# A first stage in plain fp32, a third part out of the table, a threshold on ScalarE and a split of weights at the hand-over

## The chip, the cores and the metric

The kernel runs on one core of a Trainium2 chip. The metric is the device time of a whole execution in microseconds (us), lower is better; the change is judged by medians of several runs. The engines are named as in the profile: PE is TensorE (PEld its weight loads), ACT is ScalarE, DVE is VectorE, POOL is GpSimd, SP is SyncE, which only issues DMAs.

## The reference

Three layers in a row, cut to what matters. Eight batches of 3072 tokens of width 256 run through all of them.

```
X = rfft(x, axis=1)                              # 8 x 3072 x 256
Yr = Xr @ w_r - Xi @ w_i + b_r ;  Yi = Xr @ w_i + Xi @ w_r + b_i
Yr, Yi = soft threshold by 0.01: sign(Y) * max(|Y| - 0.01, 0)
x = irfft(Yr + i Yi).reshape(24576, 256)
logits = x @ phi                                 # 32 slots
d = softmax over the tokens ; slot_input = d.T @ x
slot_out = relu(slot_input @ w1[e]) @ w2[e]      # 8 experts, 4 slots each
y = softmax over the slots(logits) @ slot_out
h = y @ w_in ; g = h * tanh(log1p(exp(h)))
out = g @ w_out                                  # 2048 hidden columns
```

## The kernel before, in words

**The trunk** computes the transforms batch by batch. A batch has four groups, so there are 32 groups `k`. `stage1` multiplies twelve chunks of 512 columns of a batch by the 128 x 128 matrix `f1`; the result goes to DRAM (`sdr`) and comes back as `bt`, regrouped. In `stage1` both factors are split into a high and a low fp32r part (`xsplit`, lines 174 to 182), and three fp32r matmuls (high x high, low x high, high x low) make one product. `stage2` multiplies `bt` by a table `tall` of 96 columns per pair of frequencies, in plain fp32: 32 matmuls a group, four to a PSUM bank. Its 96 columns are a real and an imaginary part of 48 each. ScalarE writes the high part `xh`, VectorE the low part `xl`; both also add the two parts into `xsum` and split that as a third part (lines 228 to 236). `linear` makes the complex product with three real ones of six fp32r matmuls each, from those three parts, two output halves a group. The first of the three is copied by ScalarE (`k1`), the other two are added to it by VectorE (line 257), clamped by VectorE (259) and subtracted by POOL (260): the soft threshold. `special` repeats the first product for two columns of the first group of a batch, with eight plain fp32 matmuls.

`project` multiplies by `phi` for the logits, `ptrans` turns that with TensorE transposes, `inv1` transforms back, `uturn` turns again and stores to `udr`. Once a batch the softmaxes follow (`inv2`, `smax1` to `smax3`, `csoft1`, `csoft2`) and the sums over tokens (`fwd1`, `fwd2`, `dturn`, `slots`); `ytrans` makes the transposes of the thresholded columns that `slots` needs.

**Beside the trunk** `conv` turns the 64-bit weights `w_in` and `w_out` into fp32, in 32 pieces; the 16 of `w_out` are also split into high and low and stored to `whl_d` in DRAM.

**The tail**: the experts (`Experts.run`), then `ffn`. Here 384 blocks run a pipeline: `hidden` (line 774), `gate` (Mish on ScalarE, 780), `high` and `low` (785, 789: the split of the gate's output on VectorE), and `omm` (804), which multiplies by `whl`, the split of `w_out`; `omm` follows `hidden` by `LAG` = 3 blocks.

**What sets the order**: no scheduler. Each step is put on a list with a position by `at(pos, ...)`, in units of a group; the list is sorted and the instructions issued in that order, so every engine and SP's queue work strictly in it. A position is a place in the order, not a time. `PA` and `TAIL` hold the positions; `TAIL["loads"]` those of the experts' weights. The trunk's PSUM pool has 8 banks in rotation.

Of the kernel before, what the change touches and what calls it, by code (L numbers as in the profile page):

```python
# [8 lines left out]
F32 = mybir.dt.float32  # L9
# [19 lines left out]
def constants():  # L29
# [32 lines left out]
    both = np.concatenate([t.reshape(96, -1), tt.reshape(96, -1)], axis=1)  # L62
# [4 lines left out]
def body(ctx, tc, x, w_r, w_i, b_r, b_i, phi, w1, w2, w_in, w_out, cbig, ct, out, dbg=None, stop=False):  # L67
# [16 lines left out]
    whl_d = dram.tile([2, FF, D], F32, name="whl_d")  # L84
# [28 lines left out]
    f1s = [wp.tile([128, 128], F32R, name=f"f1s{i}") for i in range(2)]  # L113
# [11 lines left out]
    def setup():  # L125
# [19 lines left out]
    def weights():
# [14 lines left out]
        nc.vector.tensor_scalar(thi, bias, -1.0, LAM, op0=ALU.mult, op1=ALU.add)  # L160

    def load_t(i, g):
        w = 8 * 96
        o = (4 * i + g) * w
        nc.sync.dma_start(out=tall[:, o:o + w], in_=ct[:, o:o + w])

    def load_x(b, j):
# [696 lines left out]
```

## Time and profile before

| | us |
|---|---|
| median of 3 runs (2008.23 to 2022.46) | 2022.21 |
| profiled execution: its own time | 2017.93 |
| its span | 2016.0 |
| PE busy in the span | 1938.5 |
| PEld busy | 1643.8 |
| DVE busy | 1310.3 |
| ACT busy | 870.0 |
| POOL busy | 271.4 |

The profiled execution is 4 us under the median and inside the spread of the runs. Matmuls overlap, so a busy PE is not PE at its peak: what a matmul takes of PE is read from the distance between starts in the timeline. A plain fp32 matmul shows as two passes there (32 for the 16 that a call of `stage2` halves issues), an fp32r matmul or a transpose as one. PEclk is the share of full clock that PE was granted.

### The profile page before, as it was taken

What the parts mean: (1) busy time and instruction counts of PE and PEld (TensorE: products, weight loads), DVE (VectorE), ACT (ScalarE), POOL (GpSimd) and SP (SyncE); (2) the same over time, 40 slices, a digit from 0 to 9 for tenths busy, and PEclk for the clock granted to TensorE, in tenths of its full rate; (3) what the DMA queues carried; (4) which work ended last, traced back from release to release, by engine and by line L of the source; (5) the groups of instructions that cost most, each with busy time, mean ns of one, the idle gap of its engine ahead of it and who ended that gap; (6) DMA issues with size and microseconds to landing.
All of it is one profiled execution on the core that took longest, in us unless ns stands there. A gap on an engine that the chain in (4) does not pass through costs nothing.

```text
span 2016.0 us, 31876 instructions
## 1 busy us (share of the span) xinstructions
PE 1938.5 (96%) x12670; PEld 1643.8 (82%) x12670; DVE 1310.3 (65%) x2026; ACT 870.0 (43%) x1563; POOL 271.4 (13%) x289
## 2 busy tenths in 40 slices
PE   5999999999999779999999999999999999999999
PEld 3887787888888638888888888888888888888887
DVE  4777777787777535666666666666666666666665
ACT  4556565566655422333333333333333333333332
POOL 1443443444534100000000000000000000000000
PEclk7989999999999989999999999999999999999999
DMA  8655565666664691001002002002002002000000
GB/s 265 175 163 148 161 170 162 177 178 175 194 175 116 204 329 27 22 22 53 22 22 53 22 21 53 11 22 53 21 22 53 22 22 53 22 22 22 22 22 21
DMA packets 148388, 177.16 MB, mean 88 GB/s; under 512 B 57600, under 2 KB 102784, under 8 KB 147984
## 3 DMA queue, kind: packets, MB, share of 16 engines
q1 hardware_dynamic: 146448, 170.38, 28.7%
q0 software_dynamic: 1792, 4.76, 0.7%
q8 instruction: 100, 1.64, 0.3%
q14 instruction: 48, 0.39, 0.1%
HBM read 103.79 MB, written 71.30 MB: 87 GB/s over the span
## 4 chain that ended last, share of the span: by engine, by line
PE 65%; DMA 3%; DVE 2%; issue 1%; ACT 1%; POOL 1%; SPq 0%; POOLq 0%; DVEq 0%; ACTq 0%
PE o L804 53%; PE h L774 9%; DMA whl<-whl_d 1%; PE l L249 1%; DMA c_d<-chl 0%; PE s L221 0%; DMA raw<-in_moe_w_dram 0%; POOL yt L260 0%; DVE xl L229 0%; PE dt L446 0%; DVE xsum L230 0%; DVE rm L343 0%; ACT xh L235 0%; DVE p L257 0%; DVE cl L259 0%
## 5 line engine op out<-in xcount | busy, mean ns | idle before, releaser
L804 PE MATMUL o<-whl,gh 128*128 128x512 f32 x3072 | 1084.8, 396 | 7.3 <-DMA whl<-whl_d 7.3
L804 PE MATMUL o<-whl,gl 128*128 128x256 f32 x3072 | 828.7, 280 | 0.0
L780 ACT ACTIVATE g<-h 128x1024 f32<-128x1024 f32 x384 | 394.3, 1027 | 759.4 <-PE h L774 753.7
L804 PEld LDWEIGHTS o<-whl,gh 128*128 128x128 f32 x3072 | 567.5, 188 | 129.7 <-issue 8.0
L804 PEld LDWEIGHTS o<-whl,gl 128*128 128x128 f32 x3072 | 579.5, 189 | 31.5
L785 DVE CAST gh<-g 128x1024 fp32r<-128x1024 f32 x384 | 265.6, 692 | 366.7 <-ACT g L780 366.7
L789 DVE TENSOR_TENSOR gl<-g,gh 128x1024 fp32r<-128x1024 f32 x384 | 469.9, 1224 | 28.9 <-DVE gh L785 0.9
L774 PE MATMUL h<-ctt,mst 128*128 128x512 f32 x768 | 241.7, 396 | 1.8 <-DVE mst L766 0.9
L260 POOL TENSOR_TENSOR yt<-p,cl 128x384 f32<-128x384 f32 x126 | 134.6, 1068 | 219.0 <-DVE cl L259 113.1
L774 PEld LDWEIGHTS h<-ctt,mst 128*128 128x128 f32 x768 | 121.4, 189 | 20.4 <-DVE mst L766 1.9
L194 PE MATMUL s<-xsp,f1s 128*128 128x512 f32 x288 | 101.9, 455 | 29.7 <-ACT xsp L177 14.7
L221 PEld LDWEIGHTS s<-tall,bt 96*128 96x128 f32 x1024 | 127.1, 203 | 3.0 <-DMA bt<-sdr 2.3
L221 PE MATMUL s<-tall,bt 96*128 96x96 f32 x1024 | 126.5, 285 | 1.8 <-DMA bt<-sdr 1.8
L812 DVE TENSOR_TENSOR os<-o,os 128x256 f32<-128x256 f32 x192 | 76.3, 418 | 76.8 <-ACT os L811 76.8
L194 PEld LDWEIGHTS s<-xsp,f1s 128*128 128x128 f32 x288 | 53.5, 203 | 53.9 <-ACT xsp L177 19.7
L259 DVE TENSOR_SCALAR cl<-p,tlo,thi 128x384 f32<-128x384 f32 x128 | 76.9, 601 | 26.0 <-POOL yt L260 15.2
L811 ACT ACTIVATE os<-o 128x256 f32<-128x256 f32 x192 | 73.7, 384 | 41.0 <-PE o L804 38.0
L257 DVE TENSOR_TENSOR p<-l,k 128x384 f32<-128x384 f32 x128 | 70.3, 549 | 24.4 <-PE l L249 23.2
L229 DVE TENSOR_TENSOR xl<-s,xh 128x384 fp32r<-128x384 f32 x128 | 70.4, 550 | 17.6 <-ACT xsum L228 16.0
L235 ACT ACTIVATE xh<-xsum 128x384 fp32r<-128x384 f32 x64 | 33.5, 524 | 100.9 <-DVE xsum L230 100.9
L224 ACT ACTIVATE xh<-s 128x384 fp32r<-128x384 f32 x128 | 62.4, 487 | 33.6 <-PE s L221 33.6
L322 ACT ACTIVATE y<-tr 96x512 f32<-96x512 f32 x128 | 66.7, 598 | 17.2 <-PE tr L320 17.2
(190 smaller groups left out, 1914.8 us busy)
## 6 DMA issues: line engine op xcount, KB each, us to landing
xc<-in_x_dram SPq DMA_DIRECT2D x96, 256.0 KB, 3.1
sdr<-a SPq DMA_DIRECT2D x96, 256.0 KB, 3.4
bt<-sdr SPq DMA_DIRECT2D x32, 768.0 KB, 7.3
out_dram<-os SPq DMA_DIRECT2D x48, 512.0 KB, 2.6
ctt<-c_d SPq DMA_DIRECT2D x32, 384.0 KB, 7.9
c_d<-chl SPq DMA_DIRECT2D x16, 384.0 KB, 3.3
w1t<-in_moe_w_dram SPq DMA_DIRECT2D x6, 1024.0 KB, 7.6
w2t<-in_moe_w_dram SPq DMA_DIRECT2D x5, 1024.0 KB, 11.0
```

Of the source, the lines that this page charges most:

```text
L194: nc.tensor.matmul(ps, lhsT=f1s[w], rhs=xs[:, v], start=n == 0, stop=n == 2)
L221: nc.tensor.matmul(ps[:, i], lhsT=b_t[k][:, p0 + i, h * 128:(h + 1) * 128], rhs=t_m[:, 8 * g + p0 + i, :], start=True, stop=True)
L229: nc.vector.tensor_sub(xl_t[k][:, h, p0:p0 + 4, 0:2], ps, xh.bitcast(F32))
L259: nc.vector.tensor_scalar(cl, p, tlo[:, ri, eh:eh + 1], thi[:, ri, eh:eh + 1], op0=ALU.max, op1=ALU.min)
L260: (nc.vector if k == NK - 1 and m == 2 else nc.gpsimd).tensor_sub(yt[:, eh, :, ri, :], p, cl)
L774: nc.tensor.matmul(ps[:, i], lhsT=mst[:, f * 128:f * 128 + 128], rhs=ct_t[b][:, 4 * m:4 * m + 4].rearrange("p n t -> p (n t)"), start=True ...
L780: nc.scalar.activation(out=g, in_=h_t.pop(p), func=AF.Mish)
L785: nc.vector.tensor_copy(gh, g)
L789: nc.vector.tensor_sub(gl, g, gh.bitcast(F32))
L804: nc.tensor.matmul(o, lhsT=a[:, i, ts], rhs=w, start=f == 0 and n == 0, stop=f == 15 and n == 1)
L811: nc.scalar.activation(out=os[:, t], in_=ps[:, 1], func=AF.Copy)
L812: nc.vector.tensor_add(os[:, t], ps[:, 0], os[:, t])
```

## The change

- The table `t_m` gets 48 more columns for each pair of frequencies, the sum of the two parts. `stage2` writes 144 columns a matmul, three to a bank (banks of 3, 3 and 2 pairs, six a group for four before), and ScalarE and VectorE split all three parts at once. `xsum` and its four instructions go.
- `stage1` is one plain fp32 matmul of `x` and `f1`; `xsplit` goes. From the second batch on `x` is loaded and the result stored in pieces of 1024 columns, at positions of their own.
- The threshold is `relu(p + b - 0.01) - relu(-p - b - 0.01)`: two ScalarE activations with a bias for each clamp of VectorE; POOL subtracts as before.
- `special` has no matmuls: its two columns ride on the first product as columns 385 and 386.
- `project` writes frequencies onto partitions in three groups of 32, and VectorE transposes 32 x 32 blocks out of PSUM, in `project` and in `inv1`; `ptrans` and `uturn` with their TensorE transposes go. `udr` is stored by four DMAs of 32 partitions for two of 96.
- `conv` loads its piece earlier, into two buffers, and no longer splits `w_out`. `w_out` is fetched as fp32 into `wof` and split into `whl` by `split`, a quarter at each of the first four even blocks of `ffn`.
- The loads of the second expert's output weights come earlier, those of the fourth and fifth behind the last store of `c_d`. The first fetch of `ctt` is cut in two around `wof`.

```diff
-    both = np.concatenate([t.reshape(96, -1), tt.reshape(96, -1)], axis=1)
+    t3 = np.concatenate([t, t[:, :, 0:48] + t[:, :, 48:96]], axis=2)
+    both = np.concatenate([t3.reshape(96, -1), tt.reshape(96, -1)], axis=1)
...
-    tall = const.tile([96, NP * 192], F32, name="tall")
-    t_m = tall[:, 0:NP * 96].rearrange("p (n f) -> p n f", f=96)
-    t_t = tall[:, NP * 96:].rearrange("p (n f) -> p n f", f=96)
+    tall = const.tile([96, NP * 240], F32, name="tall")
+    t_m = tall[:, 0:NP * 144].rearrange("p (n f) -> p n f", f=144)
+    t_t = tall[:, NP * 144:].rearrange("p (n f) -> p n f", f=96)
...
+        nc.vector.tensor_scalar(tup, bias, -LAM, None, op0=ALU.add)
...
+        w = 8 * (96 if i else 144)
+        o = NP * 144 * i + g * w
...
+        w = XC if b == 0 else 2 * XC
...
+            c = slice(j % 2 * XC, j % 2 * XC + XC)
+            xs = x_t[b, j // 2][:, c]
+            if j % 2 == 0:
+                a_t[b, j // 2] = xp.tile([128, 2 * XC], F32, tag="a", name="a")
+            a = a_t[b, j // 2][:, c]
...
-        for n, (w, v) in enumerate(((0, 0), (1, 0), (0, 1))):
-            nc.tensor.matmul(ps, lhsT=f1s[w], rhs=xs[:, v], start=n == 0, stop=n == 2)
-        if j + 1 < na:
-            xsplit(b, j + 1)
-        elif b + 1 < NB:
-            xsplit(b + 1, 0)
+        nc.tensor.matmul(ps, lhsT=f1, rhs=xs, start=True, stop=True)
...
+    def store_a(b, i):
         dst = sdr[b].rearrange("q (r n) d -> (q r) (n d)", r=4)
-        nc.sync.dma_start(out=dst[:, j * XC:(j + 1) * XC], in_=a)
+        nc.sync.dma_start(out=dst[:, 2 * i * XC:2 * (i + 1) * XC], in_=a_t.pop((b, i)))
+        x_t.pop((b, i))
...
+        n = min(3, 8 - p0)
...
-        ps = psum([128, 4, 2, 48], "s2")
-        for i in range(4):
+            xh_t[k] = bp.tile([128, 2, 3 * NC + 2], F32R, tag="xh", name="xh")
+            xl_t[k] = bp.tile([128, 2, 3 * NC + 2], F32R, tag="xl", name="xl")
+        full = psum([128, 3, 3, 48], "s2")
+        ps = full[:, 0:n]
+        for i in range(n):
...
-        xh = xh_t[k][:, h, p0:p0 + 4, 0:2]
+
+        def part(t):
+            v = t[:, h, 0:3 * NC].rearrange("p (r q f) -> p q r f", r=3, f=48)
+            return v[:, p0:p0 + n]
+
+        xh = part(xh_t[k])
         nc.scalar.activation(out=xh, in_=ps, func=AF.Copy)
-        if p0 == 0:
-            k1_t["s", h] = lp.tile([128, 8, 48], F32, tag="xsum", name="xsum")
-        xs = k1_t["s", h]
-        nc.scalar.activation(out=xs[:, p0:p0 + 4], in_=ps[:, :, 0], func=AF.Copy)
-        nc.vector.tensor_sub(xl_t[k][:, h, p0:p0 + 4, 0:2], ps, xh.bitcast(F32))
-        nc.vector.tensor_add(xs[:, p0:p0 + 4], ps[:, :, 1], xs[:, p0:p0 + 4])
+        nc.vector.tensor_sub(part(xl_t[k]), ps, xh.bitcast(F32))
         if g == 0 and p0 == 0:
-            nc.vector.tensor_copy(xs_t[k][:, h, :], ps[:, 0, 0:2, 47])
...
+            for t in (xh_t[k], xl_t[k]):
+                nc.vector.tensor_copy(t[:, h, 3 * NC:3 * NC + 2], t[:, h, 47:48 + NC:NC].bitcast(F32))
...
-        ps = psum([128, 8, 48], "l")
+        w = NC + 2 if m == 0 and k % 4 == 0 else NC
+        full = psum([128, NC + 2], "l")
+        ps = full[:, 0:w]
+        cs = slice(src * NC, src * NC + w)
...
-        nc.vector.tensor_scalar(cl, p, tlo[:, ri, eh:eh + 1], thi[:, ri, eh:eh + 1], op0=ALU.max, op1=ALU.min)
-        (nc.vector if k == NK - 1 and m == 2 else nc.gpsimd).tensor_sub(yt[:, eh, :, ri, :], p, cl)
+        nc.scalar.activation(out=cl, in_=p, func=AF.Relu, bias=tup[:, ri, eh:eh + 1])
+        nc.scalar.activation(out=p, in_=p, func=AF.Relu, scale=-1.0, bias=tlo[:, ri, eh:eh + 1])
+        (nc.vector if k == NK - 1 and m == 2 else nc.gpsimd).tensor_sub(yt[:, eh, :, ri, :], cl, p)
...
-        ps = psum([128, 2], "sp")
...
+        v = k1_t[eh][:, NC:NC + 2]
...
-        ps = psum([128, 2, 96], "pp")
+        ps = psum([96, 8, NS], "pp")
         for eh in range(2):
...
-        pt_t[k] = turn(pt_t[k], "phat")
+            v = yt[:, eh].rearrange("p q r f -> p q (r f)")
+            for a in range(3):
+                nc.tensor.matmul(ps[32 * a:32 * a + 32], lhsT=ph[:, eh, :], rhs=v[:, :, 32 * a:32 * a + 32],
+                                 start=eh == 0, stop=eh == 1, tile_position=(0, 32 * a))
+        pt_t[k] = cp.tile([96, 8, NS], F32, tag="phat", name="phat")
+        nc.vector.transpose(out=pt_t[k].rearrange("p q s -> p (q s)"), in_=ps.rearrange("p q s -> p (q s)"))
...
+        u = cp.tile([128, 2, 3, NS], F32, tag="u", bufs=2, name="u")
+        nc.vector.transpose(out=u.rearrange("p i a s -> p (i a s)"), in_=ps.rearrange("p i f -> p (i f)"))
...
+        for j in range(4):
+            q = 8 * g + 2 * j
+            nc.sync.dma_start(out=udr[b][q:q + 2].rearrange("i (a n) s -> n i a s", n=32), in_=u[32 * j:32 * j + 32])
...
+            cv["n"] = cvp.tile([128, n, 2], I32, tag="cs", bufs=2, name="cvs")
+            nc.sync.dma_start(out=cv["n"], in_=srcd[i])
...
-            nc.sync.dma_start(out=whl_d[:, 128 * i:128 * i + 128].rearrange("r p d -> p r d"), in_=cv["hl"].bitcast(F32))
...
+        for i in range(na // 2 if b else 0):
+            at(4 * b + PA["s1"] + PA["s1d"] * (2 * i + 1.5), store_a, b, i)
+            at(4 * b + PA["s1"] + PA["s1d"] * (2 * i - 2.4) if (b, i) > (1, 1) else -3.86 + 0.01 * i, load_x, b, i)
...
-            at(k + 1.02, special, k, 0)
-            at(k + 1.03, special, k, 1)
+            at(k + 0.98, special, k, 0)
+            at(k + 0.99, special, k, 1)
...
-        at(k + PA["pj"] + 0.2, ptrans, k)
-        at(k + PA["pj"] + 0.4, inv1, k)
-        at(k + PA["pj"] + 0.6, uturn, k)
+        at(k + PA["pj"] + 0.3, inv1, k)
...
-        at(sp * i - 0.02, conv, s_, d_, ii, 0)
-        for st in range(1, 7 if i < len(si) else 9):
+        at(sp * (i - 0.45), conv, s_, d_, ii, 0)
...
+            raw = big.tile([128, 24, D], F32, tag="whl", name="raw")
+            for i in range(3):
+                ex.load(2, 5 + i, None, raw[:, 8 * i:8 * i + 8])
             for h in range(2):
                 nc.sync.dma_start(out=win[:, 8 * h:8 * h + 8].rearrange("p t d -> p (t d)"), in_=win_d[128 * h:128 * h + 128])
-            c_fetch(tc, ctp, ct_t, c_d, 0)
-            load_half(1)
+            c_fetch(tc, ctp, ct_t, c_d, 0, (0, 1))
+            src = wout_d.rearrange("(t p) d -> p t d", p=128)
+            for q in range(4):
+                nc.sync.dma_start(out=wof[:, 4 * q:4 * q + 4], in_=src[:, 4 * q:4 * q + 4])
+            c_fetch(tc, ctp, ct_t, c_d, 0, (1, 4))
...
-        load_half(0)
...
-              (1.172, 1, 6, "w"), (1.173, 1, 7, "w"), (1.174, 2, 0, "w"), (1.95, 2, 1, "w"), (1.96, 2, 2, "w"), (1.97, 2, 3, "b"), (1.98, 2, 4, "b")),
+              (1.172, 1, 6, "w"), (1.173, 1, 7, "w"), (1.174, 2, 0, "w"), (1.175, 2, 1, "w"), (1.96, 2, 2, "w"), (2.25, 2, 3, "b"), (2.26, 2, 4, "b")),
...
+    def split(i):
+        hi, lo, w = whl[:, 0, 4 * i:4 * i + 4], whl[:, 1, 4 * i:4 * i + 4], wof[:, 4 * i:4 * i + 4]
+        nc.scalar.activation(out=hi, in_=w, func=AF.Copy)
+        nc.vector.tensor_sub(lo, w, hi.bitcast(F32))
...
+            if p < NPR and p % 2 == 0:
+                split(p // 2)
...
```

PE in one group in the middle of the trunk, from the projection `pp` to the next second stage, before:

```order
L277 MATMUL pp<-yt,ph 32x192 x8
L320 MATMUL tr<-cb,yt 96x128 x16
...
L287 MATMUL tn<-cb,pt 96x128 x2
...
L194 MATMUL s_2789<-xsp,f1s_113 128x512
L194 MATMUL s_2789<-xsp,f1s_114 128x512
...
L300 MATMUL iu<-tall,phat 32x96 x8
...
L287 MATMUL tn<-cb,ut 96x128 x2
...
L221 MATMUL s_2882<-tall,bt 128x96 x4
```

and in the change (`cb` holds `f1` and the identity matrix):

```order
L273 MATMUL pp<-yt,ph 32x256 x6
L299 MATMUL tr<-cb,yt 96x128 x16
...
L284 MATMUL iu<-tall,phat 32x96 x8
...
L189 MATMUL s_2325<-xc,cb 128x512
...
L218 MATMUL s_2383<-tall,bt 128x144 x3
L218 MATMUL s_2389<-tall,bt 128x144 x3
L218 MATMUL s_2395<-tall,bt 128x144 x2
```

The two turns `tn` are gone, the inverse transform `iu` stands nearer to `pp`, and the first stage has one row for three.

ScalarE around one second stage in the trunk, in the change:

```order
L250 ACTIVATE k_3040<-l 128x386
L256 ACTIVATE cl<-p,tup 128x384
L257 ACTIVATE p<-p,tlo 128x384
L193 ACTIVATE a<-s_3067 128x512
...
L226 ACTIVATE xh<-s_3085 128x3x3x48
L226 ACTIVATE xh<-s_3091 128x3x3x48
L226 ACTIVATE xh<-s_3097 128x2x3x48
```

The rows of the threshold, 256 and 257, stand ahead of the copies that empty the banks of the second stage.

SP's queue at the hand-over, from the last load of `w1` to the FFN, before:

```order
L683 DMA w1t<-in_moe_w_dram 128x2x1024 x2
L690 DMA w2t<-in_moe_w_dram 128x8x256
L415 DMA ddr<-dm 128x768
L419 DMA dd<-ddr 96x32x32
L690 DMA w2t<-in_moe_w_dram 128x8x256 x4
L405 DMA c_d_72<-chl 128x2x384 x2
...
L629 DMA win<-win_d 128x2048 x2
L646 DMA ctt<-c_d_65 32x4x768 x4
L622 DMA whl<-whl_d 128x16x256 x2
```

and in the change:

```order
L655 DMA w2t<-in_moe_w_dram 128x8x256 x2
L394 DMA ddr<-dm 128x768
L398 DMA dd<-ddr 96x32x32
L655 DMA w2t<-in_moe_w_dram 128x8x256
L384 DMA c_d_71<-chl 128x2x384 x2
L655 DMA w2t<-in_moe_w_dram 128x8x256 x2
L655 DMA raw<-in_moe_w_dram 128x8x256 x3
L595 DMA win<-win_d 128x2048 x2
L616 DMA ctt<-c_d_64 32x768 x4
L599 DMA wof<-wout_d 128x4x256 x4
L616 DMA ctt<-c_d_64 32x3x768 x4
```

The store of `c_d` stands ahead of two loads of `w2t` that it was behind, and `wof`, half the bytes of `whl`, stands ahead of most of `ctt`.

## Rows read from the trace of the kernel before

**Rows 1.** Windows by stage: length; busy us (instructions) PE, PEld, DVE, ACT, POOL; clock; DMA.

```profile
0.00:70.00 70.00, 47.74 (x176) 33.49 (x177) 37.40 (x71) 30.84 (x61) 15.02 (x19) 0.78 0.82 245
70.00:620.00 550.00, 526.80 (x4559) 449.50 (x4558) 416.68 (x860) 327.98 (x814) 234.79 (x246) 0.98 0.60 169
...
714.00:763.00 49.00, 34.61 (x253) 17.72 (x253) 14.54 (x23) 9.88 (x13) 0.00 (x0) 0.83 0.97 296
763.00:2016.00 1253.00, 1248.18 (x6892) 1078.55 (x6890) 784.78 (x952) 459.18 (x572) 0.00 (x0) 1.00 0.09 28
```

**Rows 2.** Groups of the whole span: count, busy us, mean ns, idle before, releasers.

```profile
L194 PE MATMUL s<-xsp,f1s 128*128 128x512 f32 x288 | 101.9, 455 | 29.7 <-ACT xsp L177 14.7 <-DVE xsp L178 8.2 <-POOL xsp L178 5.5
...
L194 PEld LDWEIGHTS s<-xsp,f1s 128*128 128x128 f32 x288 | 53.5, 203 | 53.9 <-ACT xsp L177 19.7 <-DVE xsp L178 16.1 <-POOL xsp L178 11.5
```

**Rows 3.** Timeline of PE, 312 to 340 us: start, duration, what, count.

```profile
312.48 0.28 PE L265 MATMUL sp<-xs,ah 128*128 128x2 f32 x2
...
314.18 0.42 PE L249 MATMUL l<-xh,bh 128*128 128x384 f32 x1
...
331.84 3.71 PE L221 MATMUL s<-tall,bt 96*128 96x96 f32 x32
335.33 0.42 PE L249 MATMUL l<-xh,ah 128*128 128x384 f32 x1
335.59 0.34 PE L249 MATMUL l<-xl,ah 128*128 128x384 f32 x1
...
336.49 0.86 PE L194 MATMUL s<-xsp,f1s 128*128 128x512 f32 x3
337.19 0.34 PE L249 MATMUL l<-xh,bh 128*128 128x384 f32 x1
337.36 0.34 PE L249 MATMUL l<-xl,bh 128*128 128x384 f32 x1
...
338.35 0.86 PE L277 MATMUL pp<-yt,ph 128*32 128x192 f32 x16
339.14 1.08 PE L320 MATMUL tr<-cb,yt 128*96 128x128 f32 x8
```

**Rows 4.** Waits of PE, whole span: us in total, times, longest.

```profile
PE pp L277 <- DVE yt L270: 3.6, 2, 1.9
...
PE tn L287 <- ACT ut L303: 2.3, 2, 2.1
PE iu L300 <- ACT phat L289: 2.0, 2, 1.6
```

**Rows 5.** Groups of the other engines, whole span, same columns as Rows 2.

```profile
L789 DVE TENSOR_TENSOR gl<-g,gh 128x1024 fp32r<-128x1024 f32 x384 | 469.9, 1224 | 28.9 <-DVE gh L785 0.9
...
L260 POOL TENSOR_TENSOR yt<-p,cl 128x384 f32<-128x384 f32 x126 | 134.6, 1068 | 219.0 <-DVE cl L259 113.1 <-PE tr L320 81.6 <-PE l L249 6.8
...
L235 ACT ACTIVATE xh<-xsum 128x384 fp32r<-128x384 f32 x64 | 33.5, 524 | 100.9 <-DVE xsum L230 100.9
...
L720 DVE COPY hs<-so 128x256 f32<-128x256 f32 x2 | 0.8, 424 | 6.4 <-PE so L717 6.4
```

**Rows 6.** Timeline of PE at the hand-over; in brackets the idle before.

```profile
722.09 5.49 PE L704 MATMUL hp<-w1t,sit 128*32 128x512 f32 x32 [3.87 <-ACT hs L706]
...
739.06 7.13 PE L761 MATMUL mp<-win,sot 128*128 128x512 f32 x16 [0.32 <-DVE sot L727]
745.89 0.77 PE L774 MATMUL h<-ctt,mst 128*128 128x512 f32 x2
...
758.65 0.77 PE L804 MATMUL o<-whl,gh 128*128 128x512 f32 x1 [7.29 <-DMA whl<-whl_d]
```

**Rows 7.** Timeline of ScalarE (ACT) at the hand-over.

```profile
721.43 1.09 ACT L706 ACTIVATE hs<-hp 128x512 f32<-128x512 f32 x2 [12.19 <-DMA c_d<-chl]
...
748.14 1.94 ACT L780 ACTIVATE g<-h 128x1024 f32<-128x1024 f32 x2
```

**Rows 8.** Timeline of PE in the first stage.

```profile
49.03 3.15 PE L194 MATMUL s<-xsp,f1s 128*128 128x512 f32 x6 [4.68 <-ACT xsp L177]
```

More of the change, by code (lines that the diff above doesn't have):

```diff
@@ L21 @@
 NP = 32
+NC = 384
 NS = 32
@@ L247, in linear @@
         for h in range(2):
-            for w, xx in ((wh, xh), (wh, xl), (wl, xh)):
-                nc.tensor.matmul(ps, lhsT=w[:, h, es], rhs=xx[:, h, :, src, :], start=n == 0, stop=n == 5)
+            for ww, xx in ((wh, xh), (wh, xl), (wl, xh)):
+                nc.tensor.matmul(ps, lhsT=ww[:, h, es], rhs=xx[:, h, cs], start=n == 0, stop=n == 5)
                 n += 1
         if m == 0:
-            k1_t[eh] = lp.tile([128, 8, 48], F32, tag="k1", name="k1")
-            nc.scalar.activation(out=k1_t[eh], in_=ps, func=AF.Copy)
+            k1_t[eh] = lp.tile([128, NC + 2], F32, tag="k1", name="k1")
+            nc.scalar.activation(out=k1_t[eh][:, 0:w], in_=ps, func=AF.Copy)
             return
@@ L273, in project @@
         yt = yt_t[k]
-        ps = psum([128, 2, 96], "pp")
+        ps = psum([96, 8, NS], "pp")
         for eh in range(2):
-            for j in range(4):
-                nc.tensor.matmul(ps[32 * j:32 * j + 32], lhsT=ph[:, eh, :],
-                                 rhs=yt[:, eh, 2 * j:2 * j + 2].rearrange("p q r f -> p q (r f)"),
-                                 start=eh == 0, stop=eh == 1, tile_position=(0, 32 * j))
-        pt = cp.tile([128, 2, 96], F32, tag="pt", bufs=2, name="pt")
-        nc.scalar.activation(out=pt, in_=ps, func=AF.Copy)
@@ L282, in project @@
-        pt_t[k] = pt
-    def turn(src, tag):
-        ps = psum([96, 2, 128], "tn")
-        for i in range(2):
-            nc.tensor.transpose(ps[:, i], src[:, i], ident)
-        t = cp.tile([96, 2, 128], F32, tag=tag, bufs=2, name=tag)
-        nc.scalar.activation(out=t, in_=ps, func=AF.Copy)
-        return t
-    def ptrans(k):
-        pt_t[k] = turn(pt_t[k], "phat")
+            v = yt[:, eh].rearrange("p q r f -> p q (r f)")
+            for a in range(3):
+                nc.tensor.matmul(ps[32 * a:32 * a + 32], lhsT=ph[:, eh, :], rhs=v[:, :, 32 * a:32 * a + 32],
+                                 start=eh == 0, stop=eh == 1, tile_position=(0, 32 * a))
@@ L570, in body @@
         sp = (NK - 1.5) / ncv
-        at(sp * i - 0.02, conv, s_, d_, ii, 0)
-        for st in range(1, 7 if i < len(si) else 9):
+        at(sp * (i - 0.45), conv, s_, d_, ii, 0)
+        for st in range(1, 7):
             at(sp * (i + st / 9), conv, s_, d_, ii, st)
-        if i >= len(si):
-            at(sp * (i + 1.3), conv, s_, d_, ii, 9)
     for z, n in TAIL["warm"]:
@@ L668, in load @@
                 src = self.w1[e][128 * h:128 * h + 128]
[L669 to L676 removed]
+                t = self.xp.tile([128, FE], F32, tag="x" if tag == "xs" else "a", name="w1t")
+                nc.sync.dma_start(out=t, in_=src)
+                parts = [t[:, 0:512], t[:, 512:FE]]
                 for q in range(2):
@@ L745, with ffn @@
 LAG = 3
-def ffn(ctx, tc, NB, mst, whl, win, c_d, out, ctp, ct_t, psh, pso, sot):
+def ffn(ctx, tc, NB, mst, whl, win, wof, c_d, out, ctp, ct_t, psh, pso, sot):
     nc = tc.nc
```

129 lines of the change are left out of this document (38 added, 91 removed).

## Prediction

> **What bounds the kernel now.** I read the span by stage first, then the rows of PE, then the waits. By stage [rows 1] the FFN takes 1253.0 of 2016.0 us with PE busy 1248.2; the chain of waits says the same of its matmuls. The change does not touch them: the eight new split instructions run in its first blocks, beside ScalarE and VectorE that are idle for most of this stage. So all that can move is the 763 us before. In the body, 70 to 620 us, PE is busy 526.8 of 550.0: it is PE-bound with 23.2 us of idle. In the first 70 us PE is busy 47.7 and the DMA engines 0.82; at the hand-over, 714 to 763, PE is busy 34.6 of 49.0 and the DMA engines 0.97. Three prices count, then: what PE has to issue in the body, what it waits for there, and what ends the two transitions.
>
> What one matmul costs PE is read from starts in the timeline [rows 3], not from its duration. 32 passes of 96 columns in the second stage take 335.33 - 331.84 = 3.49 us, 0.109 each. 16 passes of 2 columns in `special` take 314.18 - 312.48 = 1.70, 0.106 each: a plain fp32 pass over a full set of weights has a floor of about 0.11 us, whatever its columns. At 512 columns, `mp`, 16 passes take 745.89 - 739.06 = 6.83 [rows 6], 0.427 each, 0.834 ns a column. Three fp32r matmuls of 512 columns take 0.70 (336.49 to 337.19), and the first `linear` matmul after plain fp32 takes 0.26 where it takes 0.17 after fp32r (335.33 to 335.59, 337.19 to 337.36).
>
> **The change, part by part.** Minus is a gain.
>
> *First stage.* 96 chunks: two passes of 0.427 for 0.70 is +0.154 each, +14.8 us. Of these 84 stand in the trunk between `linear` matmuls, which then start after plain fp32: 84 x 0.09 = +7.6. The split on ScalarE, VectorE and POOL goes, and with it what PE waited for. The matmul row [rows 2] was idle 29.7: 14.7 for ScalarE's part, nearly all in the first stage, 8.2 for VectorE's and 5.5 for POOL's. The weight loads of the same line waited 16.1 + 11.5 for the latter two. The gain in the body lies between 13.7 and 27.6; I take 18, since a wait of the loads hides partly behind running matmuls.
>
> *The 48 columns.* Nothing shows a pass of 144 columns. Below it cannot be under the floor of 0.109; in proportion to 96 columns it would be 0.164. The nearest row is the long pass: 144 x 0.834 = 0.120, over the floor. 1024 passes x 0.011 = +11.3, ends 0 and +56. Six banks a group in place of four are filled, with the same elements to drain and without the partial sums; the pool has eight, so I price that among the new waits.
>
> *`special`.* 128 passes x 0.106 = -13.6. Two more columns in sixteen products are nothing beside 384.
>
> *The turns.* 128 transposes: the eight of 128 columns at 339.14 last 1.08 [rows 3], less some 0.28 for the last one's end about 0.114 apart: -14.6. 64 pairs of them no longer stand before `linear`, 64 x 0.09, though not all did: -5. In their place VectorE transposes 256 columns and 192 from PSUM, 64 times. No row has that operation; the nearest is a PSUM copy of 256 columns, 0.424 [rows 5], the far end a subtraction of 1024 columns, 1.22. 56 of them in the body are 24 to 68 us on an engine that is busy 416.7 of 550.0 [rows 1] and loses the clamps, the partial sums and the split of `x`. They hide, unless PE comes to the inverse transform first; 0.3 of a group, some 6 us, is left for that. The Trainium skill prices it (VectorE: DVE Perf Modes, "The three transpose paths" and the rules for kernel authors: a full 128 x 128 transpose belongs on TensorE, VectorE only turns blocks of 32 x 32, 311 ns for 128 columns); two of those would be an estimated 0.62 us a call, no run here shows it, and the sum would be the same.
>
> *`project`.* Now 16 passes of 192 columns, four abreast, take 339.14 - 338.35 = 0.79, so four rounds of 0.160 and 0.15 around them. Twelve passes of 256 three abreast are again four rounds, of 0.213: 1.00. 32 x 0.21 = +6.8.
>
> PE's work together: 14.8 + 7.6 + 11.3 - 13.6 - 14.6 - 5 + 6.8 = **+7.3**.
>
> *Other waits that go.* `pp` for `special`'s result 3.6, the turn for its copy 2.3, `iu` for the other copy 2.0 [rows 4]: 7.9, part of which returns as waits for VectorE's transposes; I take -6, ends -7.9 and 0.
>
> *New waits.* ScalarE gets eight activations of 384 columns a group. At 0.524 (the SBUF to SBUF row of that size [rows 5]) that is 4.2 us. The body holds about 27.4 groups of 20.1 us, so ScalarE's 328.0 are 12.0 a group, and even without crediting a copy it loses, it has 16.2. Behind a threshold that waits stand the copies that empty the second stage's banks, and PE waits for those; eight banks are several us of PE's work. I take +4, ends 0 and +14. The ends take in `conv`'s, `x`'s and `u`'s DMAs as well: SP's queue gets 12 DMAs a batch for `x` and its result in place of 24, and 16 for `u` in place of 8.
>
> *Clock.* PE was granted 0.98 in the body [rows 1], so it spent about 4% of 550 us at 1.2 and not 2.4 GHz, and lost 11 us by it. With fewer long waits of PE part of it returns: -4, ends -11 and 0.
>
> *First stage of all.* PE no longer waits for the copy of `x`, 4.68 us at one place [rows 8], of 14.7. Against it: the table is 0.59 MB larger (48 columns x 32 x 96 rows x 4 bytes), at 245 GB/s [rows 1] 2.4 us, and the second stage now stands behind three matmuls on pieces of 0.52 MB that are loaded after the first table parts, 4.3 us for two. I take -3, ends -8 and +7.
>
> *Hand-over.* The experts' second half waited 3.87 for ScalarE's `hs`, which itself waited 12.19 for a store of `c_d` [rows 6, 7]; that store moves ahead of two loads of 1 MB. Then 7.29 for `whl`: `omm` began at 758.65. Now `whl` is made on the chip. ScalarE's first gate starts at 748.14, two take 1.94 [rows 7]; with one split of 1024 columns between, the second ends at 751.1, and VectorE's low half and first gate split follow at 1.22 or less each [rows 5]: `omm` can start near 752, 6.6 earlier. 3.9 + 6.6 = -10.5, ends 0 and -12.
>
> **Sum**: 7.3 - 18 - 6 + 4 - 4 - 3 - 10.5 = -30, against 2017.93: **1988 us**. The median of the runs shown is 4 us higher and their spread 14, so the same figure stands for the median.
>
> **Rivals.**
> *A, the hand-over stays bound by transfers* (DMA 0.97 there [rows 1]): 1988 + 10.5 = 1998. Against it, 2 MB fewer are moved, some 7 us at 296 GB/s.
> *B, the columns cost in proportion*: (0.164 - 0.120) x 1024 = +45, 2033, no change. Against it stand 2 columns at the price of 96.
> *C, ScalarE becomes the bound, slower.* It has 16.2 of 20.1 us a group, and each of four thresholds can hold it: for VectorE's addition (some 0.5) and, as `cl` has one buffer, for POOL's subtraction before, 1.07 [rows 5]. If all four do in full, 16.2 + 4 x 1.6 = 22.6 us, and 31 groups are 2.5 longer: 1988 + 77 = 2065. It decides from 20.1 on, that is from 1 us of holding each; against it, POOL's subtraction of the threshold before is usually long over, with 3 us between them. The Trainium skill is on this side (ScalarE: Activation LUTs, "Rules for kernel authors": maximum, minimum and relu belong on VectorE); its 280 ns plus 0.833 ns a column with a bias from memory is an estimated 0.60 us for each, 4.8 a group, no run here shows it, and C would then be 2083.
> *D, nearly all waits go*: the load rows' 27.6, the other 7.9, no new ones, the whole 11 of the clock, 8 in the first stage: 27 more, 1961.
> *E, new waits of the size of the old* (24) eat the body's gain: 2008, no change.
> That the change does not do what it says is no case: the rows of the order show each part of it.
>
> **How the numbers follow.** My case, 1968 to 2002, has 0.50; A 0.13, D 0.12, E 0.11, B 0.06, C 0.08. One per cent, about what a measurement of this kernel can tell from no change, is 20 us: faster is under 2002. That gives faster 0.75 (mine, A, D), same 0.17 (B, E), slower 0.08 (C). The range 1960 to 2012 leaves out B, C and half of D, 0.20.
>
> **What would show it.** Passes of the second stage at 0.120 apart, first-stage chunks at 0.85; no wait of PE on a first-stage matmul in the body; PE still busy 0.95 of it; the group near 19.5 us; ScalarE under 0.75 busy in the body; `omm` starting some 6 us after the first `h`. PE waiting for ScalarE's copies or POOL's `yt` in each group would make it wrong, and so would a first second stage that starts over 5 us later than at present.

## The result and the profile after

The changed kernel takes 2030.36 us (median of 10 runs, 2024.27 to 2032.68) against 2019.33 (10 runs): a ratio of 1.0062, interval 1.0042 to 1.0083, 8 to 17 us slower. Forecast were 1988 and a range of 1960 to 2012, so the sign was wrong. The profiled execution (2029.12 us, span 2027.3) by stage, columns as in [rows 1]:

```profile
0.00:70.00 70.00, 43.99 (x178) 28.66 (x179) 21.10 (x45) 21.37 (x39) 9.45 (x16) 0.85 0.88 264
70.00:620.00 550.00, 516.99 (x4073) 415.09 (x4072) 297.16 (x660) 349.71 (x710) 164.91 (x193) 0.97 0.57 160
620.00:730.00 110.00, 88.12 (x748) 67.99 (x750) 52.58 (x112) 57.62 (x118) 21.49 (x24) 0.91 0.51 154
730.00:775.00 45.00, 39.83 (x315) 20.73 (x308) 16.77 (x29) 11.82 (x15) 0.00 (x0) 0.88 0.91 271
775.00:2027.00 1252.00, 1247.18 (x6886) 1077.59 (x6884) 788.00 (x955) 460.61 (x574) 0.00 (x0) 1.00 0.09 28
```

No engine but PE is near its limit in the body (70 to 620 us): ScalarE is 0.64 busy. Yet PE is idle 33.0 of 550 us there, where it was idle 23.2 [rows 1]. The change took much work off VectorE and POOL and the waits grew.

PE's timeline gives marks that both kernels have. Each line is the time from the mark above it, us:

| to | before | after | difference |
|---|---|---|---|
| first `linear` matmul | 55.9 | 55.2 | -0.7 |
| that of group 25 | 501.9 | 500.7 | -1.2 |
| last `linear` matmul | 115.5 | 132.5 | +17.0 |
| experts' first matmul (`hp`) | 41.2 | 48.2 | +7.0 |
| first `h` | 31.3 | 25.4 | -5.9 |
| first `o` | 12.8 | 6.1 | -6.6 |
| end | 1257.4 | 1259.3 | +1.9 |

The hand-over gained 12.5 us, 2 more than forecast. The body gained nothing, and its end and the last softmax chain lost 24 us. What PE, and then ScalarE, waited for from 70 to 620 us (us in total, times, longest):

```profile
PE mt L329 <- DVE rm L324: 10.3, 5, 2.8
PE pp L273 <- DVE yt L265: 10.3, 5, 3.4
PE tn L435 <- ACT dtt L428: 5.5, 6, 2.1
PE lps L314 <- DMA v<-udr: 3.0, 2, 2.0
...
ACT cl L256 <- DVE p L254: 69.9, 72, 2.5
ACT xh L226 <- DVE xl L227: 63.0, 85, 1.0
ACT cl L256 <- POOL yt L258: 12.6, 19, 1.1
ACT xh L226 <- DVE xh L230: 11.1, 13, 2.3
```

Nearly all of PE's waits lie where a batch ends: the softmax maximum (`mt`), the projection that needs the special columns, the turn of `dtt`. ScalarE is busy 349.7 us and stands another 157 in these four rows: it waits before one operation, and all that stands behind it in its queue is held up too. The first two rows of ScalarE are the two halves of the story: `cl`, the threshold, waits for VectorE's sum; `xh`, the copy of a second-stage piece, waits for VectorE's subtraction of the piece before.

One batch end shows it. PE's timeline, then ScalarE's, in brackets the idle before and what ended it:

```profile
313.61 1.45 PE L314 MATMUL lps<-v,cb 128*128 128x384 f32 x4
314.90 1.02 PE L189 MATMUL s<-xc,cb 128*128 128x512 f32 x2
315.85 0.62 PE L273 MATMUL pp<-yt,ph 128*32 128x256 f32 x2
317.97 1.19 PE L273 MATMUL pp<-yt,ph 128*32 128x256 f32 x10 [1.50 <-DVE yt L265]
319.10 1.95 PE L299 MATMUL tr<-cb,yt 128*96 128x128 f32 x16
323.00 0.30 PE L329 MATMUL mt<-cb,rm 128*128 128x128 f32 x1 [1.96 <-DVE rm L324]
...
315.57 0.41 ACT L226 ACTIVATE xh<-s 128x288 fp32r<-128x288 f32 x1 [0.74 <-DVE xl L227]
317.71 0.49 ACT L250 ACTIVATE k<-l 128x384 f32<-128x384 f32 x1 [1.73 <-DVE cs L264]
319.07 0.62 ACT L256 ACTIVATE cl<-p,tup 128x384 f32<-128x384 f32 x1 [0.87 <-DVE p L254]
319.72 0.62 ACT L257 ACTIVATE p<-p,tlo 128x384 f32<-128x384 f32 x1
320.24 0.85 ACT L315 ACTIVATE lg<-lps 128x384 f32<-128x384 f32 x2
```

The logits (`lps`) leave PE by 315.06. Their copy `lg` starts at 320.24, behind four operations of ScalarE, three of which waited for VectorE first; the maximum and PE's `mt` follow. From 324.0 to 330.8 PE's granted clock is then 0.50, the lower level of 1.2 GHz.

### The profile page after: what moved, and what is told of

Read it like the earlier page. It is cut to its first block, busy times and chain, and to the rows that moved or that the text cites. A ratio compares the mean times of both kernels' runs of the same rounds, so it can differ in the third digit from the quotient of the medians.

```text
span 2027.3 us, 30318 instructions
## 1 busy us (share of the span) xinstructions
PE 1936.1 (95%) x12190; PEld 1610.1 (79%) x12190; DVE 1175.6 (58%) x1799; ACT 901.1 (44%) x1455; POOL 195.8 (10%) x231
## 4 chain that ended last, share of the span: by engine, by line
PE 79%; ACT 7%; DVE 6%; DMA 3%; issue 2%; POOL 1%; SPq 1%; ACTq 0%; POOLq 0%; DVEq 0%
PE o L774 53%; PE h L744 9%; PE l L246 6%; PE s L218 3%; DVE xl L227 3%; PE s L189 3%; ACT xh L226 2%; ACT cl L256 1%; ACT p L257 1%; DMA xc<-in_x_dram 1%; PE sps L446 1%; ACT y L301 1%; DMA ctt<-c_d 1%; POOL yt L258 1%; PE tr L299 1%
## 5 line engine op out<-in xcount | busy, mean ns | idle before, releaser
L774 PEld LDWEIGHTS o<-whl,gl 128*128 128x128 f32 x3072 | 579.6, 189 | 32.4 <-DVE gl L759 1.0
L227 DVE TENSOR_TENSOR xl<-s,xh 128x432 fp32r<-128x432 f32 (+1 forms) x192 | 106.0, 558 | 159.7 <-ACT xh L226 159.6
L258 POOL TENSOR_TENSOR yt<-cl,p 128x384 f32<-128x384 f32 x126 | 127.8, 1014 | 413.8 <-ACT p L257 258.9
L226 ACT ACTIVATE xh<-s 128x432 fp32r<-128x432 f32 (+1 forms) x192 | 90.4, 488 | 97.3 <-DVE xl L227 73.5
L218 PEld LDWEIGHTS s<-tall,bt 96*128 96x128 f32 x1024 | 129.5, 190 | 4.7 <-issue 3.9
L189 PE MATMUL s<-xc,cb 128*128 128x512 f32 x192 | 106.8, 652 | 26.0 <-DMA xc<-in_x_dram 26.0
L218 PE MATMUL s<-tall,bt 96*128 96x144 f32 x1024 | 130.7, 286 | 0.0
L254 DVE TENSOR_TENSOR p<-l,k 128x384 f32<-128x384 f32 x128 | 70.9, 554 | 97.3 <-PE l L246 65.5
L256 ACT ACTIVATE cl<-p,tup 128x384 f32<-128x384 f32 x128 | 78.9, 616 | 103.9 <-DVE p L254 83.3
L781 ACT ACTIVATE os<-o 128x256 f32<-128x256 f32 x192 | 73.5, 383 | 41.1 <-PE o L774 38.1
L257 ACT ACTIVATE p<-p,tlo 128x384 f32<-128x384 f32 x128 | 78.8, 616 | 4.1
L193 ACT ACTIVATE a<-s 128x512 f32<-128x512 f32 x90 | 52.8, 589 | 42.4 <-PE s L189 42.4
```

Source lines behind the costliest of these rows:

```text
L189: nc.tensor.matmul(ps, lhsT=f1, rhs=xs, start=True, stop=True)
L227: nc.vector.tensor_sub(part(xl_t[k]), ps, xh.bitcast(F32))
L256: nc.scalar.activation(out=cl, in_=p, func=AF.Relu, bias=tup[:, ri, eh:eh + 1])
L258: (nc.vector if k == NK - 1 and m == 2 else nc.gpsimd).tensor_sub(yt[:, eh, :, ri, :], cl, p)
L774: nc.tensor.matmul(o, lhsT=a[:, i, ts], rhs=w, start=f == 0 and n == 0, stop=f == 15 and n == 1)
```

## The experiments

Ratios are to the kernel before, run beside each, with 95% intervals. Its median was 2020 us beside the first four runs, 2019 beside the next four and 2014 beside the last four, so times from different sets compare to some 6 us only. The edits are shown shortened.

First the four parts that the traces made suspects, each undone in the changed kernel.

**Pieces laid out pair by pair.**

```
-  xh_t[k] = bp.tile([128, 2, 3 * NC + 2], F32R, ...)      # r, q, f
+  xh_t[k] = bp.tile([128, 2, 8, 3, 48], F32R, ...)        # q, r, f
+  (special columns: 6 matmuls of 2 columns from a small tile)
```

> The changed kernel with the second stage's split tiles laid out pair by pair again (8 x 3 x 48), so that the six pieces of a group no longer interleave in memory; the two special columns become matmuls of 2 columns from a small tile. Theory 1 (the interleaving makes ScalarE's copy of each piece wait for VectorE's subtraction of the piece before, 0.73 us each, and this late drain is what PE waits for at each batch boundary): those waits vanish, first copy to last subtraction takes 4.0 to 4.6 us in place of 6.25, PE's wait at `project` in the body falls from 10.3 us to under 5, and the time falls by 5 to 12 us, to 2018 to 2025. Rival (the drain is off the path; the boundary waits come from the order of PE's own work): the drain shortens as said, but the time stays within 3 us of 2030.

Measured: 1988.42, ratio 0.9847 [0.9829, 0.9866]. ScalarE's copies, columns as in [rows 2]; in the changed kernel they were idle 97.3, 73.5 of it for `xl`:

```profile
L227 ACT ACTIVATE xh<-s 128x432 fp32r<-128x432 f32 (+1 forms) x192 | 77.6, 497 | 1.7 <-PE s L220 1.5
```

The interleaved layout did make each copy wait, and that drain was on the path: 42 us, more than three times the 12 that the theory gave it at most. PE's wait at `project`, 10.3 us in the body of the changed kernel, is gone. That the kernel's scheduling layer orders accesses by address range is inferred from this, not shown further.

**Threshold back on VectorE.**

```
-  nc.scalar.activation(out=cl, in_=p, func=AF.Relu, bias=tup)
-  nc.scalar.activation(out=p, in_=p, func=AF.Relu, scale=-1.0, bias=tlo)
-  POOL: yt = cl - p
+  nc.vector.tensor_scalar(cl, p, tlo, thi, op0=ALU.max, op1=ALU.min)
+  POOL: yt = p - cl
```

> The changed kernel with the threshold back on VectorE (one clamp) and POOL (one subtraction). Theory 1 (ScalarE at 0.64 busy in the body is not what holds PE; the threshold there costs only some 2 us, at the last group): 2026 to 2032. Rival C of the prediction in a milder form (two more operations of 0.62 us per threshold with one buffer for the clipped value hold PE all over the body and the last groups): 2012 to 2020.

Measured: 1977.06, ratio 0.9791 [0.9770, 0.9813], 53 us under the changed kernel. My first theory fell, and even the rival's price was too low. The threshold on ScalarE is the dearest part of the change.

**Weight loads at their old places.**

```
-  (1.175, 2, 1, "w"), (1.96, 2, 2, "w"), (2.25, 2, 3, "b"), (2.26, 2, 4, "b")
+  (1.95, 2, 1, "w"), (1.96, 2, 2, "w"), (1.97, 2, 3, "b"), (1.98, 2, 4, "b")
```

> The changed kernel with the experts' second-layer weight loads at their old places, one of 1 MB behind the last softmax chain again. Theory 1 (the moved load is in flight with the last batch's two short transfers, which took 10.4 us in place of 7.8, and PE then ran `sps` at 1.2 GHz): store and load of the last batch take 7.5 to 8.5 us, the last softmax chain to the experts shortens by 4 to 7 us, and the time falls by 3 to 7 us, to 2023 to 2027. Rival (the chain shortens but the weights come later by as much, so that the experts or the first FFN block wait): 2028 to 2032.

Measured: 2025.57, ratio 1.0024 [1.0010, 1.0039], 5 us gained as the first theory said. In the profiles the last softmax chain up to `hp` takes 40.7 us for 48.2. Store and load of the last `ddr` take 6.9 us (706.52 to 713.46) in place of 10.4 (712.34 to 722.72). But a wait comes back that the change had removed [rows 6]:

```profile
PE hp L669 <- ACT hs L671: 3.7, 1, 3.7
```

**Second batch's first stage behind two second stages.**

```
+  def S1(b, j):
+      return 0.03 + 0.16 * j if b == 1 else 4 * b + PA["s1"] + PA["s1d"] * j
```

> The changed kernel with the first stage of the second batch (12 chunks, their loads and stores) placed behind the second stage of the first two groups, in place of three chunks ahead of it. Theory 1 (PE reaches the second stage at 44.3 us only because it stands in order behind chunks whose input lands at 39.1 and 40.9, while its own input landed at 31.9): the second stage starts at 32 to 34 us, the first linear matmul at 40 to 44 in place of 55.2, and the time falls by 6 to 12 us, to 2018 to 2024. Rival (the transfers of the table and of the second batch set the pace of the first 100 us anyway; the wait moves to `project` or to the second batch's second stage): 2027 to 2033.

Measured: 2019.10, ratio 1.0013 [0.9995, 1.0031], 11 us gained, as the first theory said. The second stage starts at 32.4 us, the first linear matmul at 43.0.

With my theory of the threshold gone, the next runs asked how it costs 53 us, and what the first stage alone is worth.

**Subtractions behind the copies**, layout unchanged.

```
-  nc.vector.tensor_sub(part(xl_t[k]), ps, xh.bitcast(F32))
+  late.append((part(xl_t[k]), ps, xh.bitcast(F32)))
+  if p0 == 6:                  # third piece of the half
+      for xl_, ps_, xh_ in late:
+          nc.vector.tensor_sub(xl_, ps_, xh_)
```

> The changed kernel with one thing moved: VectorE's three subtractions of a half group stand behind ScalarE's three copies, so that no copy has to wait for the subtraction of the piece before it. Theory 1 (that wait, 0.73 us four times a group, delays all that stands behind it on ScalarE): ScalarE's waits at the copies vanish without the extra small matmuls that the laid-out version paid for (96 of them, some 0.11 us each, 10 us), so 1974 to 1984 where that one had 1988. Rival (three banks are now held until ScalarE is through, and PE waits for banks instead): 2000 to 2030.

Measured: 2001.25, ratio 0.9907 [0.9880, 0.9934], at the lower end of the rival's range, but not for the rival's reason: no matmul of the second stage waited for a bank. The copies' wait went, but the sums now stand behind three subtractions in a row and ScalarE waits for them longer, 107.2 us in place of 69.9 in the body:

```profile
ACT cl L259 <- DVE p L257: 107.2, 74, 3.6
```

**Threshold handed over one product later.**

```
   nc.vector.tensor_add(p, ps, k1)
+  flush()                      # the threshold of the product before
+  late.append((k, eh, m, ri, p, yt))
```

> The changed kernel with both rectifications of a threshold handed to ScalarE one linear product later, behind the next product's copy, with the same number of operations on every engine. Theory 2 (it is not ScalarE's busy time but its standing in order before VectorE's addition, 26.0 us in 12 groups, that makes the copies behind it late): that wait falls below 6 us in 12 groups, PE's waits at the batch boundary with it, and the time is 1980 to 1998. Rival (4.9 us more of ScalarE's time a group is what counts): 2020 to 2032.

Measured: 2041.89, ratio 1.0114 [1.0085, 1.0143]. Missed by both: ScalarE's wait for the sum is gone (2.0 us left in the body), but the result comes later and the projection had no slack for it:

```profile
PE pp L283 <- POOL yt L268: 34.4, 20, 2.6
```

**First stage alone, on the kernel before.**

```
-  for n, (w, v) in enumerate(((0, 0), (1, 0), (0, 1))):
-      nc.tensor.matmul(ps, lhsT=f1s[w], rhs=xs[:, v], ...)
+  nc.tensor.matmul(ps, lhsT=f1, rhs=xs, start=True, stop=True)
```

> The kernel before with the first stage alone in plain fp32, in one matmul a chunk from the loaded input, without the split of the input. Theory 1 (PE pays 0.147 us for each of 96 chunks, 14 us, and saves 9.2 us of waits in the body, some 3 us at the lower clock and a few in the first stage): 2014 to 2024 against 2020. Rival (the operations that leave ScalarE, VectorE and POOL, 96 of each kind, make their other work arrive earlier too, so that the waits of the batch boundaries shrink as well): 1998 to 2012.

Measured: 1983.68, ratio 0.9832 [0.9802, 0.9862], past even the rival. The body, as in [rows 1]:

```profile
70.00:620.00 550.00, 548.03 (x4708) 453.66 (x4707) 389.55 (x879) 314.91 (x777) 191.92 (x226) 1.00 0.63 175
```

PE's idle time falls from 23.2 to 2.0 us and its clock is whole. Not only the waits for the split vanish (9.2 us in the body), but nearly all the others. That ScalarE, VectorE and POOL reach their other work earlier without the split is the likely reason; no run tests it by itself.

**Four edits together** (threshold on VectorE, subtractions behind copies, old load places, new order of the head).

> The changed kernel with four edits together: threshold on VectorE, the subtractions behind the copies, the weight loads at their old places, the second batch's first stage behind the second stage of two groups. Theory 1 (the first two remove the same waits, the last two work at other places): 1977 - 5 - 11 and up to 4 less for the order, 1957 to 1963. Rival (with the body shorter, transfers become late, and the earlier start is waited off): 1965 to 1975.

Measured: 1961.62, ratio 0.9715 [0.9689, 0.9741], as the first theory said; it beats both kernels.

**ScalarE's time given back as idle work** (threshold on VectorE).

```
+  for _ in range(2):
+      nc.scalar.activation(out=dum, in_=k1_t[eh][:, 0:NC], func=AF.Relu, bias=tlo)
```

> The changed kernel with the threshold on VectorE (1977 us), and ScalarE given back its two activations of 384 columns per threshold, but as idle work: they read the first product's copy, which is long there, and write a scratch tile that nobody reads. Theory 2 (what costs is that ScalarE stands in order before VectorE's sum, and that the threshold's result comes later): ScalarE's busy time is back within 5% of the changed kernel's, and the time stays at 1975 to 1988. Theory 3 (4.9 us more a group in ScalarE's queue are enough to make its copies late): 2008 to 2030.

Measured: 1979.61, ratio 0.9825 [0.9794, 0.9855]. ScalarE is busier in the body than in the changed kernel, 378.9 us against 349.7, and PE hardly notices: it is busy 537.3 us, 537.2 without the idle work.

```profile
70.00:620.00 550.00, 537.29 (x4348) 436.41 (x4347) 383.18 (x835) 378.87 (x762) 177.76 (x207) 1.00 0.60 166
```

So ScalarE's busy time is not the cost. What is left is that each threshold stands before VectorE's sum, and that its own result comes later; this run does not part the two.

**Threshold on ScalarE alone, on the kernel before.**

```
-  nc.vector.tensor_scalar(cl, p, tlo, thi, op0=ALU.max, op1=ALU.min)
-  POOL: yt = p - cl
+  nc.scalar.activation(out=cl, in_=p, func=AF.Relu, bias=tup)
+  nc.scalar.activation(out=p, in_=p, func=AF.Relu, scale=-1.0, bias=tlo)
+  POOL: yt = cl - p
```

> The kernel before with the threshold alone as two rectifications on ScalarE. Theory (the threshold on ScalarE costs about as much without the other parts; ScalarE was 328 of 550 us busy in this body and gets 4.9 us a group more): 30 to 60 us more than before, 2050 to 2080. Rival (it costs only beside the interleaved pieces of the changed kernel, at which ScalarE waits too): 2015 to 2030.

Measured: 2107.02, ratio 1.0463 [1.0429, 1.0496]: 93 us, more than forecast, and in this kernel no copy of a piece waits for the subtraction of the piece before, so the threshold does not need that to cost time. PE waits for ScalarE's copies at the turns, in 14 and in 10 of the body's 24 groups:

```profile
ACT cl L261 <- DVE p L259: 75.5, 56, 4.0
...
PE tn L290 <- ACT pt L284: 29.1, 14, 3.3
PE iu L303 <- ACT phat L292: 16.5, 10, 4.8
```

**One product later, and the projection later too.**

```
-  at(k + PA["pj"], project, k)
-  at(k + PA["pj"] + 0.3, inv1, k)
+  at(k + PA["pj"] + 0.17, project, k)
+  at(k + PA["pj"] + 0.47, inv1, k)
```

> The changed kernel with both rectifications one linear product later, as in the run that came to 2042, and now the projection and the inverse transform 0.17 of a group later too, so that the later result is not waited for. Theory 2: PE's wait at the projection for POOL's result falls from 34.4 us in the body to under 10, ScalarE does not wait for VectorE's sum, and the time is 1985 to 2005. Rival (theory 3, ScalarE's time is what counts, or the later projection is then late for the inverse transform and the softmax chain): 2022 to 2045.

Measured: 1989.30, ratio 0.9868 [0.9837, 0.9900]. With the same operations on the same engines as the changed kernel it is 41 us faster (39 by the ratios): neither wait is left, ScalarE's for the sum nor PE's for POOL. So most of the 53 us is order, not work. What the later projection would give by itself is not shown, since no run moves it alone; PE's largest wait in the body is now for the load behind the inverse transform (`lps` for `v`, 8.7 us).

**Turns back on TensorE** (threshold on VectorE).

```
-  nc.vector.transpose(out=phat, in_=ps)    # and the same for u
+  pt: copy by ScalarE; two nc.tensor.transpose; copy by ScalarE
```

> The changed kernel with the threshold on VectorE (1977 us), and the turns back on TensorE with ScalarE's copies, and the projection in 16 passes of 192 columns. The prediction's terms (14.6 + 5 us of transposes against 6.8 for the projection, all on PE's path): 1985 to 1995. Rival (the transposes on VectorE make the inverse transform later by as much as PE saves): 1972 to 1980.

Measured: 1980.51, ratio 0.9820 [0.9788, 0.9851], against 0.9791 [0.9770, 0.9813] with them on VectorE. The intervals overlap: the turns on VectorE are worth some 3 to 6 us, not clear of nothing, nearer to the rival than to the terms. The turned tiles have one buffer in this run and two in the kernel before; what that costs is not shown.

## Why the prediction was wrong

**The step that failed is "New waits": +4, ends 0 and +14.** It put ScalarE's threshold at 4.2 us of its time in a group that this would fill to 16.2 of 20.1, and took room for safety. The measured cost is 53 us. The wait that it named is not there: the second stage's matmuls were never idle (L218 below, 0.0), so PE did not wait for their banks. It waited at the batch ends, in the rows `mt`, `pp` and `tn` above. Rival C had the mechanism, that each threshold holds ScalarE's queue for VectorE's addition and POOL's subtraction, with an end of 2065 and a chance of 0.08; what ScalarE waited for was mostly the addition, 69.9 us in the body, and little the subtraction, 12.6. What was wrong in weighing it was the point from which it decides: 20.1 us, the group full. At 0.64 busy it already cost 53 us, since some copies in ScalarE's queue are awaited within a few us: `lg`, `dtt`, and the second stage's pieces, behind which VectorE makes the special columns.

Without that one part the changed kernel takes 1977.06, inside the range and 11 us from the forecast, but in part by luck: other terms were off too, in both directions, as shown below. Rival B's 2033 lies near the measured time by luck as well, since its passes of 0.164 took 0.120 to 0.122. Of the signs that were named, the passes, the chunks, the first stage's waits and `omm` came out as said; the group did not, 20.4 us for 19.5 (244.4 for 12 groups).

The Trainium skill (ScalarE: Activation LUTs, "Rules for kernel authors") has relu, maximum and minimum on VectorE, and was right on the side. The estimate of 0.60 us, worked out from that page's price, agrees with the row of the threshold, 0.616. The page's reason, speed per element, is not what counted: the run with idle work paid the same 0.615 us twice for each threshold and lost 3 to 7 us, within overlapping intervals.

```profile
L218 PE MATMUL s<-tall,bt 96*128 96x144 f32 x1024 | 130.7, 286 | 0.0
L256 ACT ACTIVATE cl<-p,tup 128x384 f32<-128x384 f32 x128 | 78.9, 616 | 103.9 <-DVE p L254 83.3 <-POOL yt L258 19.5 <-POOL cvc L478 1.1
L276 DVE STREAM_TRANSPOSE phat<-pp 96x256 f32<-96x256 f32 x32 | 14.0, 437 | 1.3 <-PE pp L273 1.3
L287 DVE STREAM_TRANSPOSE u<-iu 128x192 f32<-128x192 f32 x32 | 12.1, 378 | 6.2 <-PE iu L284 5.9
```

**The waits were counted beyond what was there.** -18, -6 and -4 for clock took 24 us of idle from a stage that had 23.2 [rows 1], and 18 of it from rows of the whole span [rows 2], of which 20.1 us lay in the first 70 us. The body's own waits at that line were 9.2:

```profile
PE s L194 <- DVE xsp L178: 5.0, 3, 3.2
PE s L194 <- POOL xsp L178: 3.3, 2, 1.9
PE s L194 <- DVE xsum L230: 0.9, 1, 0.9
```

The right question was what makes the copies late. The first stage alone points to it: its terms summed to 14.8 + 7.6 - 18 - 3 = +1.4, and it is worth 36 us, since 21 of the body's 23 us of waits and the 0.02 of clock go with it. So the two largest parts were misjudged by 49 and 37 us, in opposite directions, and much of the one hid the other.

**"Six banks with the same elements to drain"** missed the new layout. The drain of a group, from the first copy to the last subtraction, takes 6.25 us for six pieces (from 337.01 to 343.26); VectorE alone needs 6 x 0.56 = 3.4.

```profile
337.01 0.52 ACT L226 ACTIVATE xh<-s 128x432 fp32r<-128x432 f32 x1
342.81 0.46 DVE L227 TENSOR_TENSOR xl<-s,xh 128x288 fp32r<-128x288 f32 x1 [0.54 <-ACT xh L226]
```

Undoing it gave 42 us, but not on top of the 53: with the threshold on VectorE, the subtractions moved and 16 us of other edits the time is 1961.62, no less than 1977 without those 16. Each wait by itself costs PE little. With the threshold on VectorE ScalarE still waits for `xl`, in the body no less than in the changed kernel (first row below), and PE is busy 537.2 of 550 us; with the pieces laid out pair by pair it waits even longer for `p` (second row), and PE is busy 539.2.

```profile
ACT xh L226 <- DVE xl L227: 70.3, 86, 2.5
ACT cl L260 <- DVE p L258: 97.2, 87, 2.8
```

So a sum of ScalarE's waits does not say what they cost. The two in one queue cost the time; in the kernel before, where the threshold alone cost 93 us, that queue had waits of its own (for `xsum`, 49.8 us in the body of that run).

**PE's work** was the better part. A pass of 144 columns takes 0.120 to 0.122 (32 from 552.07 to 555.90, 32 from 44.28 to 48.20), forecast 0.120. A first-stage chunk between linear products:

```profile
339.44 1.02 PE L189 MATMUL s<-xc,cb 128*128 128x512 f32 x2
339.90 0.74 PE L246 MATMUL l<-xh,bh 128*128 128x384 f32 x1
340.48 0.34 PE L246 MATMUL l<-xl,bh 128*128 128x384 f32 x1
340.65 0.33 PE L246 MATMUL l<-xh,bl 128*128 128x384 f32 x1
340.82 0.34 PE L246 MATMUL l<-xh,bh 128*128 128x384 f32 x1
```

From the chunk's start to that of the fourth product after it are 1.38, which would be three products of 0.177 without it: the chunk costs 0.85, as forecast. The switch charge of 7.6 us is not there: the later first start (0.58) is the chunk's own second pass. In 12 groups (from 292.8 and from 294.8) the lengths are 245.2 and 244.4 and PE's idle time 10.4 and 11.1, at the same clock of 0.99: some 1.5 less work, where 7.3 x 12 / 32 = 2.7 more was forecast. The turns gave 3 to 6 of their 12.8: their price on VectorE, 0.44 and 0.38, was well placed, and PE is idle 12.8 us in the body with them there and 11.0 with them on TensorE. Where the rest went is not shown.

**The end of the body** was not priced at all. PE was busy 117.0 of 132.5 us there where it was busy 111.1 of 115.5, the clock 0.92 for 0.99. The last groups have no first stage left, so that PE has less to do between a result and its use; that this is why is argued, not shown. It is no cause of its own: with the threshold on VectorE this stretch takes 114.0 us, with the pieces laid out pair by pair 114.7. Of the 57 us between the profiled executions of the changed kernel and of the one with the threshold on VectorE, 34 lie before this stretch, 18.5 in it and 4 in the last softmax chain.

**A load that moves** was named only for the hand-over. The moved 1 MB flies beside the last batch's store and load, `ddr` and `dd`. From issue to landing the store took 6.5 us, 3.2 with the loads at their old places, the load 3.7 and 3.6:

```profile
722.85 1.13 PE L425 MATMUL dt<-tall,dd 96*32 96x96 f32 x32 [3.63 <-DMA dd<-ddr]
...
728.01 6.37 PE L446 MATMUL sps<-y,dh 96*32 96x256 f32 x64
...
736.55 7.07 PE L669 MATMUL hp<-w1t,sit 128*32 128x512 f32 x64 [0.32 <-DVE sit L573]
...
755.12 7.13 PE L726 MATMUL mp<-win,sot 128*128 128x512 f32 x16 [0.32 <-DVE sot L692]
761.95 0.77 PE L744 MATMUL h<-ctt,mst 128*128 128x512 f32 x2
...
768.08 0.79 PE L774 MATMUL o<-whl,gh 128*128 128x512 f32 x1 [0.18 <-DVE gh L755]
```

After that wait `sps` runs 6.37 us, at a mean granted clock of 0.56, where with the loads at their old places it took 3.66. The same rows show the hand-over: `hp` has lost its wait of 3.87, and `o` starts 6.1 us after the first `h` (12.8 before): -5.9 and -6.6, where -10.5 together was forecast.

**The first stage of all** gave -0.7, forecast -3. Its sign, a second stage more than 5 us later, was met (44.3 against 35.5), and the run that undid it gained 11 us.

## What to carry to other kernels

Before an operation goes to another engine, list what stands behind it in that engine's queue and who waits for that: an engine that is 0.64 busy can still be the one that all wait for. Take the waits of a stage from that stage, never more than its idle time, and ask whether they have one common cause, as they seem to have had in the first stage's split here. A tile whose pieces interleave can tie two engines into turns; look for a constant gap before each piece. Here it cost time only together with the threshold in the same queue.

## What the runs showed of the hardware that was not expected

A VectorE transpose of 96 x 256 fp32 from PSUM takes 0.437 us, of 128 x 192 0.378. The Trainium skill's 311 ns for 128 columns of bf16 (VectorE: DVE Perf Modes, "The three transpose paths") gave an estimate of 0.62 for the first; the measurement decides. A plain fp32 chunk of 512 columns among fp32r products costs 0.85 us and nothing for the change of kind, against 0.70 for three fp32r passes. A store and a load of 384 KB in a row on the last chain took 7.8 us in the kernel before and 6.9 in the run with the loads at their old places, and 10.4 with one load of 1 MB more in flight.
